# Loading the late slots' rows as runs with SP and turning them on VectorE, instead of gathering them with GpSimd and turning them on TensorE, in a fused attention and mixture-of-experts kernel

## The chip, the cores and the metric

The kernel runs on one core of one Trainium2 chip. The metric is device time in microseconds of one execution. The kernel before took 610.86 us (median of 3 runs, 610.16 to 613.93). The engines are called PE (TensorE matmuls; PEld is its weight load), DVE (VectorE), ACT (ScalarE), POOL (GpSimd) and SP (SyncE, which here only issues DMAs).

## The reference

Linear attention gives 4608 tokens of 512 features. Each token goes to one of 8 experts, the one with the largest cosine similarity, and gets that expert's two-layer network times its gate weight.

```
def _moe_ref(x, expert_emb, tau, w1, w2):
    ...                                   # xn, en: rows over their norms
    logits = xn @ en.T / tau
    expert_idx = np.argmax(logits, axis=1)
    ...                                   # probs: softmax of logits
    gate_w = probs[np.arange(N), expert_idx]
    for e in range(E):
        mask = expert_idx == e
        ...
        h = np.maximum(x[mask] @ w1[e], 0.0)
        out[mask] = gate_w[mask, None] * (h @ w2[e])
```

Here N is 4608, D 512, E 8 and F 1024: W1 of an expert is 512x1024, W2 1024x512, 2 MB each in 4-byte numbers.

## The kernel before, in words

**Two halves.** The first half computes attention and routing for four groups of 1152 tokens. Each token's 512 features, its number and its gate weight (514 words, `DX`) are scattered by POOL into a DRAM table `x_by_e`, in which every expert owns a stretch of `CAP` rows (L689 `scatter`). While that goes on, six early slots of 256 tokens each run through an expert; a list of step names written out by hand (`ORDER`) sets the order there. What the early slots don't take is worked off in late slots of up to 384 tokens (3 tiles of 128), one expert each. With this routing there are ten late slots: seven of 3 tiles and three of fewer, which run the 2-tile code. Their loop is at L1139; all engines run through it in program order, with branches on the slot's count of tokens.

**One late slot `s`**, in the order of the loop:
- `fetch` (L884) of the next slot: `tokens` (L897) has POOL gather the next slot's 384 rows from the table with three indirect DMAs, by a list of places computed ahead; `weights1` (L910) has SP load the next expert's W1 in four column chunks of 512 KB. Each chunk's DMA waits until the chunk before it in that buffer has been split.
- `hidden` (L1156), once as 3-tile and once as 2-tile code, takes four chunks `c` of 256 hidden units: `split2` (W2's chunk into a high and a low part: ACT casts, DVE subtracts), then `ffn1` (L953): 24 matmuls on PE, then the ReLU's high part on ACT (`hh`, L969) and its low part on DVE (`hl`, L971). Every product is done as three matmuls: high by high, high by low, low by high.
- `prepare` (L1166): the next slot's token numbers, SP's loads of the next W2, and `prepx` (L942): 12 PE transposes of 128x128 that turn the gathered rows so that features lie on partitions, then the split of these into `xh` (ACT) and `xl` (DVE). Then `split1` of the next W1: chunks 0 and 1 here, 2 and 3 after the first tile of `ffn2`.
- `ffn2` (L976), per tile: 24 matmuls into one PSUM bank, in the order of the chunks `c`, so that chunk 3's `hh` and `hl` are read by the last six; ACT scales by the gate weight (`ob`, L993) and POOL scatters the rows to the output (L995).

**Around the first late slot**, `last_early` (L1098) does the same by hand for the last early slot: a matmul `spread` broadcasts the places, four DVE instructions (`late_places`, L822) make the list, POOL gathers, PE turns.

Rows of the table behind an expert's last token have never been written; the gather skips them through an index out of range.

Of the kernel before, what the change touches and what calls it, by code (L numbers as in the profile page):

```python
# [9 lines left out]
F32 = mybir.dt.float32  # L10
# [12 lines left out]
E, F = 8, 1024  # L23
# [7 lines left out]

DX = DM + 2
TS = 3
T = TS * P
CAP = N
ROWS = E * CAP
# [24 lines left out]

PAD_LEFT, PAD_RIGHT, PAD_LATE = 88, 184, 176

# [58 lines left out]
lp9.3 lp10.3 lp11.3 x5l0.4 sc2.3 lp12.3 lp13.3 x5l1.4 sc3.3 lp14.3 lp15.3 lp16.3 lp17.3 sc4.3 lp18.3 ob41.4 lp19.3  # L122
lp20.3 lp21.3 lp22.3 sc5.3 lp23.3 lp24.3 lp25.3 lp26.3 sc6.3 lp27.3 lp28.3 lp29.3 lp30.3 lp31.3 sc7.3 lp32.3 lp33.3
sc8.3 od41.4 right.4
# [4 lines left out]
def attention_moe(ctx, tc, q, k, v, emb, tau, w1, w2, out):  # L129
# [44 lines left out]

    x_by_e = dram.tile([ROWS, DX], I32, name="x_by_e")

# [6 lines left out]
    for m, n in ((const, PAD_LEFT), (att["right"], PAD_RIGHT)):  # L183
        POOL.memset(m.tile([P, n], F32, name="pad"), 0.0)
    lower = const.tile([P, P], F32, name="lower")
    half = const.tile([P, GT], F32, name="half")
# [562 lines left out]
    def late_plan():  # L749
# [22 lines left out]
        total = t([1], "total", I32)  # L772
        start_count = t([2, n], "start_count")
        over = const.tile([P, n, TS], U32, name="late_over")
        place = const.tile([P, n, TS], U32, name="late_place")
# [3 lines left out]
        def spread():  # L779

            b["t"] = ps.tile([P, 2, n], F32, tag="t", name="spread")
            PE.matmul(b["t"], ones[:n, :], start_count, start=True, stop=True)
            b["st"], b["ct"] = (b["t"][:, k].unsqueeze(2).broadcast_to([P, n, TS]) for k in range(2))

        plans[-1] = (lambda k, i: par[i : i + 1, k : k + 1], [place, over], total[0:1])
        chain(NG - 1, "lp", [
# [23 lines left out]
            lambda: DVE.tensor_scalar(ft, ft, 0.0, float(P), ALU.max, ALU.mult),  # L810
            lambda: DVE.tensor_scalar(par[:, 0:1], es, float(E - 1), None, ALU.min),
            lambda: DVE.tensor_tensor(ct, ct, ft[:, 1:2], ALU.min),
            lambda: DVE.tensor_tensor(st, st, ft[:, 0:1], ALU.add),
            lambda: DVE.tensor_tensor(ct, ct, ft[:, 0:1], ALU.subtract),
            lambda: DVE.tensor_scalar(bad, es, float(E), float(2 * ROWS), ALU.is_ge, ALU.mult),
            lambda: DVE.scalar_tensor_tensor(ct, bad, -1.0, ct, ALU.mult, ALU.add),
            lambda: DVE.tensor_scalar(par[:, 1:2], ct, 0.0, None, ALU.max),
            lambda: DVE.tensor_scalar(start_count[:, 0], ident[:n, :n], st, None, ALU.mult),
            lambda: DVE.tensor_scalar(start_count[:, 1], ident[:n, :n], ct, None, ALU.mult),
            lambda: DVE.tensor_copy(total, cum[:, E - 1 : E]),  # L820
        ])
        def late_places():  # L822
# [4 lines left out]

        return spread, late_places


    w1f = w1.rearrange("e d f -> (e d) f")
    w2f = w2.rearrange("e f d -> (e f) d")
    raws, w1h, w1l, w2h, w2l, h_t, xs_t, xg_t = [], [], [], [], [], {}, {}, {}
    def h_room(m, name, n):
# [26 lines left out]
    def late_room():  # L861


        close_room("h_early")
        close_room("right")
        m = open_room("late", "right")
        h_room(m, "l", T)
        for i in range(2):
            x_room(m, i, T)
        r2 = [m.tile([P, FC // P, DM], F32, name=f"r2_{c}") for c in range(2)]  # L870
        for i in range(2):
            xg_t[i] = m.tile([P, TS, DX], F32, name=f"xg_{i}")
        raws.append([m.tile([P, NC1, FC], F32, name=f"r1_{c}") for c in range(NF)])
        raws.append(r2 + [m.tile([P, FC // P, DM], F32, name=f"r2_{c}") for c in range(2, NF)])
        DVE.memset(m.tile([P, PAD_LATE], F32, name="pad_late"), 0.0)
        DVE.memset(xg_t[0], 0.0)
# [7 lines left out]
    def fetch(s, plan, i):  # L884
# [3 lines left out]
        ix, xg = ix_t[s % 3][:, :nt], xg_t[set_of(s)]  # L888
        r1, r2 = [[None] * NF, [None] * NF] if s < EARLY else raws

# [6 lines left out]
        def tokens():  # L897
            for j in range(nt):
# [4 lines left out]
                tc.add_to_no_dep_group("gather", ins.ins)  # L903

        def numbers():
# [20 lines left out]
        return ix, xg, r1, r2, (tokens, numbers, weights1, weights2)  # L926

# [14 lines left out]
    def prepx(s, js, got, xs):  # L942

        xg, ts_ = got[1], slice(js[0] * P, (js[-1] + 1) * P)
        xh, xl = (x[:, :, ts_] for x in xs)
        pt = ps.tile([P, NC1, len(js) * P], F32, tag="t" if len(js) == 1 else "x", name=f"pt{s}_{js[0]}")
        for i, j in enumerate(js):
            for c in range(NC1):
                PE.transpose(pt[:, c, i * P : (i + 1) * P], xg[:, j, c * P : (c + 1) * P], ident)  # L949
        yield  # L950
        yield from split(pt, xh, xl)

    def ffn1(s, nt, xs, c):  # L953
# [144 lines left out]
    def last_early():  # L1098

        s, got, gn = EARLY - 1, gots[EARLY - 1], fetch(EARLY, plans[-1], 0)  # L1100
        tokens, numbers, weights1, weights2 = gn[4]
        weights1()
# [10 lines left out]
        go(2, first[0])  # L1113
        spread, places = late_places
        spread()
# [3 lines left out]
        places()  # L1119
        tokens()  # L1120
        go(1, first[0])
        go(2, first[1])
# [7 lines left out]
        for _ in range(3):  # L1130
            go(1, *x)
        DVE.memset(xg_t[1], 0.0)
        go(3, *second)
# [4 lines left out]
    with ExitStack() as ifs:  # L1138
        for s in range(EARLY, SLOTS):  # L1139
# [26 lines left out]
            def prepare(cs, x):  # L1166
                if not last:
                    with late(i + 1):  # L1168
# [44 lines left out]
```

## Time and profile before

| | |
|---|---|
| time, median of 3 runs | 610.86 us |
| time of the profiled execution | 612.98 us |
| its span, first to last instruction | 611.2 us |
| mean granted TensorE clock | 0.963 |
| PE busy | 544.4 us (89%) |
| DVE busy | 330.3 us (54%) |
| ACT busy | 280.2 us (46%) |
| POOL busy | 198.5 us (32%) |
| DMA, mean over the span | 177 GB/s |

How to read the profile: a row of the timeline is start, duration, engine, line, operation, output and input tile, and in brackets how long the engine had been idle before it and what ended that. Matmuls overlap (the next starts before the last has ended), so the pace of PE is read from the starts, not from durations. A row of groups gives count, total busy time, mean duration in nanoseconds, and the idle time before the group. The chain of waits is followed back from the last instruction. Names such as `xg`, `pt`, `w1l`, `ph` are the program's tiles: gathered rows, their transposes in PSUM, W1's low part, `ffn1`'s result in PSUM.

### The profile page before, as it was taken

How to read it: one execution, taken by the hardware profiler on the slowest of the kernel's cores; microseconds unless marked ns; L12 is line 12 of the kernel's file. 1: busy time of each engine (PE TensorE's matmuls, PEld its weight loads, DVE VectorE, ACT ScalarE, POOL GpSimd, SP SyncE). 2: the span in 40 equal slices, each digit the busy share in tenths (PEclk: the TensorE clock that was granted, in tenths of full speed). 3: DMA queues.
4: the chain of work that ended last, by engine and by line, in shares of the span. 5: the costliest groups of instructions: out<-in, count | busy, mean ns of one | idle time of the engine just before them, and what ended most of it. 6: DMA issues, size and time to landing. Idle time of an engine off the chain costs nothing. (4 is left out here: it accounts for less than half of the span.)

```text
span 611.2 us, 13218 instructions
## 1 busy us (share of the span) xinstructions
PE 544.4 (89%) x5170; PEld 489.3 (80%) x5170; DVE 330.3 (54%) x597; ACT 280.2 (46%) x420; POOL 198.5 (32%) x189
## 2 busy tenths in 40 slices
PE   0485627999999999997999999999999999999995
PEld 0364626988888988896998988989898999989894
DVE  5987658783475624763453656624445353624450
ACT  2767536713567414613353646534344352534340
POOL 2645425675514564161403121021130303022111
PEclk9988776999999999998999999999999999999998
DMA  9954875478623422048835576555555535454100
GB/s 321 396 214 157 296 241 174 136 283 247 240 81 115 148 90 103 3 187 310 273 126 178 178 245 196 177 185 189 179 172 159 186 127 176 150 187 159 46 18 31
DMA packets 61043, 108.16 MB, mean 177 GB/s; under 512 B 4350, under 2 KB 29982, under 8 KB 60960
## 3 DMA queue, kind: packets, MB, share of 16 engines
q1 hardware_dynamic: 51600, 78.65, 38.6%
q0 software_dynamic: 9280, 28.40, 12.8%
q8 instruction: 51, 0.84, 0.6%
q14 instruction: 32, 0.26, 0.1%
q10 hardware_dynamic: 80, 0.02, 0.0%
HBM read 89.71 MB, written 19.44 MB: 179 GB/s over the span
## 5 line engine op out<-in xcount | busy, mean ns | idle before, releaser
L995 POOL DMA_INDIRECT out_dram<-ob,ix x38 | 39.2, 1031 | 268.3 <-ACT ob L993 237.8
L964 PE MATMUL ph<-x,w1h 128*128 128x384 f32 (+1 forms) x320 | 102.2, 320 | 2.3 <-ACT ob L993 1.4
L966 PE MATMUL ph<-x,w1l 128*128 128x384 f32 (+1 forms) x320 | 102.1, 319 | 0.0
L965 PE MATMUL ph<-x,w1h 128*128 128x384 f32 (+1 forms) x320 | 102.1, 319 | 0.0
L931 DVE TENSOR_TENSOR w2l<-r,w2h 128x1024 fp32r<-128x1024 f32 x44 | 53.9, 1224 | 72.8 <-ACT w2h L929 72.8
L986 PE MATMUL po<-w2h,h_l 128*128 128x512 f32 x224 | 89.3, 399 | 0.1
L987 PE MATMUL po<-w2l,h_l 128*128 128x512 f32 x224 | 88.1, 393 | 0.0
L988 PE MATMUL po<-w2h,h_l 128*128 128x512 f32 x224 | 88.0, 393 | 0.0
L931 DVE TENSOR_TENSOR w1l<-r,w1h 128x1024 fp32r<-128x1024 f32 x48 | 57.0, 1220 | 39.0 <-ACT w1h L929 39.0
L993 ACT ACTIVATE ob<-po,ix 128x512 f32<-128x512 f32 x38 | 26.1, 687 | 106.9 <-PE po L988 58.0
L971 DVE SCALAR_TENSOR_TENSOR h_l<-ph,h_l 128x768 fp32r<-128x768 f32 (+1 forms) x44 | 37.8, 861 | 63.8 <-ACT h_l L969 63.1
L969 ACT ACTIVATE h_l<-ph 128x768 fp32r<-128x768 f32 (+1 forms) x44 | 32.2, 734 | 86.0 <-issue 62.8
L964 PEld LDWEIGHTS ph<-x,w1h 128*128 128x128 f32 x320 | 60.5, 189 | 3.4 <-ACT ob L993 1.7
L929 ACT CAST w1h<-r 128x1024 fp32r<-128x1024 f32 x48 | 48.4, 1050 | 28.9 <-DMA r<-in_moe_w_dram 28.9
L965 PEld LDWEIGHTS ph<-x,w1h 128*128 128x128 f32 x320 | 60.5, 189 | 0.3
L966 PEld LDWEIGHTS ph<-x,w1l 128*128 128x128 f32 x320 | 60.5, 189 | 0.0
L964 PE MATMUL ph<-x_e,w1h 128*128 128x256 f32 x192 | 55.9, 291 | 0.1
L965 PE MATMUL ph<-x_e,w1h 128*128 128x256 f32 x192 | 54.4, 283 | 0.0
L929 ACT CAST w2h<-r 128x1024 fp32r<-128x1024 f32 x48 | 50.0, 1043 | 9.5 <-PE po L988 4.1
L966 PE MATMUL ph<-x_e,w1l 128*128 128x256 f32 x192 | 54.2, 283 | 0.0
L988 PEld LDWEIGHTS po<-w2h,h_l 128*128 128x128 f32 x224 | 42.6, 190 | 9.2
L986 PEld LDWEIGHTS po<-w2h,h_l 128*128 128x128 f32 x224 | 42.7, 190 | 8.9 <-issue 0.3
(275 smaller groups left out, 1020.0 us busy)
## 6 DMA issues: line engine op xcount, KB each, us to landing
r<-in_moe_w_dram SPq DMA_DIRECT2D x96, 512.0 KB, 4.4
q<-in_q_dram SPq DMA_DIRECT2D x8, 1152.0 KB, 6.2
v<-in_v_dram SPq DMA_DIRECT2D x8, 1152.0 KB, 11.1
k<-in_k_dram SPq DMA_DIRECT2D x7, 1152.0 KB
k<-in_k_dram SPq DMA_DIRECT2D x1, 640.0 KB, 5.4
out_dram<-ob,ix POOLq DMA_INDIRECT x38, 3.2
x_by_e<-x,posu POOLq DMA_INDIRECT x36, 4.7
k<-in_k_dram SPq DMA_DIRECT2D x1, 512.0 KB, 3.9
```

The lines of the kernel that those rows point to most:

```text
L929: ACT.copy(hi, src)
L931: eng.tensor_tensor(lo, src, hi.bitcast(F32), ALU.subtract)
L964: PE.matmul(o, w1h[c][:, d, fs], xh[:, d, :n], start=d == 0, stop=False)
L965: PE.matmul(o, w1h[c][:, d, fs], xl[:, d, :n], start=False, stop=False)
L966: PE.matmul(o, w1l[c][:, d, fs], xh[:, d, :n], start=False, stop=d == NC1 - 1)
L969: ACT.activation(hh[c][:, :, :n], ph[:, :, :n], AF.Relu)
L971: DVE.scalar_tensor_tensor(hl[c][:, :, :n], ph[:, :, :n], 0.0, hh[c][:, :, :n].bitcast(F32), ALU.max, ALU.subtract)
L986: PE.matmul(po, hh[c][:, u, ts_], w2h[c][:, u, :], start=c + u == 0, stop=False)
L987: PE.matmul(po, hh[c][:, u, ts_], w2l[c][:, u, :], start=False, stop=False)
L988: PE.matmul(po, hl[c][:, u, ts_], w2h[c][:, u, :], start=False, stop=c + u == NC2 // 2)
L993: ACT.activation(ob, po, AF.Copy, scale=ix[:, j, 1:2].bitcast(F32))
L995: ins = POOL.indirect_dma_start(out, bass.IndirectOffsetOnAxis(ap=ix[:, j, 0:1], axis=0), ob, None, bounds_check=N - 1, oob_is_err=False,)
```

## The change

The gathers and the PE transposes of all late slots but the first go. In their place:
- `pieces`: SP loads the next slot's rows as they lie, from the first row's place (read into a register), in four DMAs. DMA `c` takes words 128c to 128c+127 of all 384 rows and puts them on partitions 32c to 32c+31, row 32n+r on partition 32c+r, as 12 runs of 512 bytes per partition. A fifth DMA loads the token numbers and gate weights, 8 bytes per row. Then come W1's loads, also in four blocks of 32 partitions with runs of 4 KB (`weights1_parts`), in the order of features that the turned rows have. W1's chunk buffers are now views of one tile, so each of these DMAs waits until all four chunks are split.
- `turnx`: DVE transposes blocks of 32x32, 8 of 12 block columns in chunk 3 of `hidden`, ahead of `ffn1`'s chunk 3, the other 4 in `prepare`; both are then split by ACT and DVE as before, from SBUF instead of PSUM.
- `pad`: since rows behind an expert's end are now read, POOL writes them, two slots ahead, with three indirect DMAs per slot whose other rows are skipped by an index out of range. The table gets 384 more rows per expert and at its end. The list of these places takes four more DVE instructions in the plan, one more small matmul, and four DVE instructions in `last_early` (`behind_places`).

```diff
-CAP = N
+CAP = N + T
...
+        def pad():
+            for j in range(nt):
+                ins = POOL.indirect_dma_start(
+                    x_by_e, bass.IndirectOffsetOnAxis(ap=plan[3][:, i, j : j + 1], axis=0),
+                    early_rows[:, 0].bitcast(I32), None, bounds_check=ROWS + T - 1, oob_is_err=False,
+                )
...
+        def pieces():
+            at = row_at()
+            for c in range(NQ):
+                ins = SP.dma_start(
+                    xq_t[0][c * QB : (c + 1) * QB].bitcast(I32),
+                    at[:, c * P : (c + 1) * P].rearrange("(n r) x -> r n x", r=QB),
+                )
+            ins = SP.dma_start(ix.bitcast(I32), at[:, DM:DX].rearrange("(j p) x -> p j x", p=P))
...
+        def weights1_parts():
+            e = expert()
+            for c in range(NQ):
+                SP.dma_start(
+                    r1_all[c * QB : (c + 1) * QB],
+                    w1f[ds(e * DM, DM), :].rearrange("(q d r) f -> q r d f", q=NQ, d=NC1)[c],
+                )
...
+    def turnx(s, nt, ns, xs):
+        rows = xq_t[0][:, ns.start : ns.stop]
+        ...
+        DVE.transpose(
+            xt.rearrange("p k (n c) -> p n k c", c=QB), rows.rearrange("p n (k r) -> p n k r", r=QB)
+        )
+        yield
+        yield from split(xt, xh, xl)
...
         places()
         tokens()
+        behind_places()
+        fetch(EARLY + 1, plans[-1], 1)[4][4]()
...
-        DVE.memset(xg_t[1], 0.0)
...
-                    gn[4][0]()
-                    gn[4][2]()
+                    gn[4][5]()
+                    gn[4][7]()
+                    if i + 2 < NMAX:
+                        fetch(s + 2, plans[-1], i + 2)[4][4]()
...
                 for c in range(NF):
                     run(split2(c, got))
+                    if c == NF - 1 and not last:
+                        run(turnx(nxt, nt, slice(0, 8), xs_t[set_of(nxt)]))
                     run(ffn1(s, nt, xs, c))
...
-                            gn[4][1]()
                             gn[4][3]()
-                            run(*(prepx(nxt, js, gn, xs_t[set_of(nxt)]) for js in ((0, 1), (2,))))
+                            run(turnx(nxt, TS, slice(8, 12), xs_t[set_of(nxt)]))
                         run(*(split1(c, gn) for c in cs))
+                        if not x:
+                            gn[4][6]()
```

In the last lines `gn[4][0]` is `tokens`, `[1]` `numbers`, `[2]` `weights1`, `[3]` `weights2`, `[4]` `pad`, `[5]` `pieces`, `[6]` `tails` (one DVE instruction that masks the token numbers) and `[7]` `weights1_parts`.

**DVE, at the end of `hidden` and in `prepare` of the first late slot, 2-tile code.** `h_l` with input `ph` is `hl`; `x_37..` is `xl` of the next slot. Before:

```order
L931 TENSOR_TENSOR w2l_718<-r_3_3727,w2h_722 128x1024
L971 SCALAR_TENSOR_TENSOR h_l<-ph_2_3_4190,h_l 128x2x256
L1161 UNCONDITIONAL_BRANCH
L907 TENSOR_TENSOR ix_113<-xg_3721,late_over 128x3
L908 COPY ix_113<-xg_3721 128x3
L931 TENSOR_TENSOR x_3717<-pt_0_4226,x_3717 128x4x256
L931 TENSOR_TENSOR x_3717<-pt_2_4237,x_3717 128x4x128
L931 TENSOR_TENSOR w1l_707<-r_0_3722,w1h_711 128x1024
```

and now:

```order
L991 TENSOR_TENSOR w2l_719<-r_3_3729,w2h_723 128x1024
L1019 STREAM_TRANSPOSE xt_20_4217<-xq 128x8x4x32
L991 TENSOR_TENSOR x_3722<-xt_20_4217,x_3722 128x4x256
L1043 SCALAR_TENSOR_TENSOR h_l<-ph_2_3_4221,h_l 128x2x256
L1238 UNCONDITIONAL_BRANCH
L1019 STREAM_TRANSPOSE xt_38_4255<-xq 128x4x4x32
L991 TENSOR_TENSOR x_3722<-xt_38_4255,x_3722 128x4x128
L991 TENSOR_TENSOR w1l_708<-r_3727,w1h_712 128x1024
```

A transpose and the larger subtraction for `xl` have moved ahead of chunk 3's `hl`; the cast for `xh` has moved ahead of chunk 3's `hh` on ACT in the same way.

**SP, at the top of the same slot.** Before:

```order
L1146 TENSOR_LOAD p_par
L892 TENSOR_LOAD p_par
L915 ISA
L915 DMA r_0_3722<-in_moe_w_dram 128x4x256
L915 ISA
L915 DMA r_1_3723<-in_moe_w_dram 128x4x256
```

and now (the `xq` and `r_3727` rows come four times each):

```order
L1219 TENSOR_LOAD p_par
L925 TENSOR_LOAD p_par
L946 ISA
L946 DMA xq<-x_by_e 32x12x128
...
L951 DMA ix_114<-x_by_e 128x3x2
L911 TENSOR_LOAD p_par
L974 ISA
L974 DMA r_3727<-in_moe_w_dram 32x4x1024
```

Five more DMAs and one more register load stand ahead of W1's four on SP; W2's four follow as before.

**DVE in `last_early`, with the waits that the program sets.** DMASW is a semaphore that a DMA issued by POOL raises. Before:

```order
L825 TENSOR_TENSOR late_place<-number,spread 128x60
L826 TENSOR_TENSOR late_place<-late_place,late_over 128x60 [waits DVE_49]
L971 SCALAR_TENSOR_TENSOR h_l<-ph_2_0_3738,h_l 128x2x256 [waits DMAHW1_49,Activation_49]
L971 SCALAR_TENSOR_TENSOR h_l<-ph_2_1_3765,h_l 128x2x256 [waits Activation_49]
L931 TENSOR_TENSOR w1l_707<-r_0_3722,w1h_711 128x1024 [waits DMAHW6_49,Activation_49]
```

and now:

```order
L834 TENSOR_TENSOR late_place<-late_place,late_over 128x60 [waits DVE_49]
L838 TENSOR_TENSOR xq<-number,spread 128x60 [waits DMASW4_49,DMASW5_49,DMASW3_49,DMASW6_49,DMASW2_49,DMASW7_49,DMASW1_49,DMASW0_49]
L839 TENSOR_SCALAR xq<-xq 128x60 [waits DVE_49]
L840 TENSOR_TENSOR late_behind<-number,spread 128x60
L841 TENSOR_TENSOR late_behind<-late_behind,xq 128x60 [waits DVE_49]
L1043 SCALAR_TENSOR_TENSOR h_l<-ph_2_0_3740,h_l 128x2x256 [waits DMAHW1_49,Activation_49]
```

The first of the four new instructions waits for DMAs that POOL issued, and `hl` of chunks 0 and 1 now stands behind it.

More of the change, by code (lines that the diff above doesn't have):

```diff
@@ L172, in attention_moe @@
         open_room(name, side)
-    x_by_e = dram.tile([ROWS, DX], I32, name="x_by_e")
+    x_by_e = dram.tile([ROWS + T, DX], I32, name="x_by_e")
     ident = const.tile([P, P], F32, name="ident")
@@ L184, in attention_moe @@
         POOL.memset(m.tile([P, n], F32, name="pad"), 0.0)
+    behind = const.tile([P, NSLOT, TS], U32, name="late_behind")
     lower = const.tile([P, P], F32, name="lower")
@@ L779, in spread @@
         def spread():
[L781 to L785, printed above, removed]
+            b["t"] = ps.tile([P, 3, n], F32, tag="t", name="spread")
+            PE.matmul(b["t"][:, :2], ones[:n, :], start_count, start=True, stop=True)
+            PE.matmul(b["t"][:, 2], ones[:n, :], left_n, start=True, stop=True)
+            b["st"], b["ct"], b["left"] = (b["t"][:, k].unsqueeze(2).broadcast_to([P, n, TS]) for k in range(3))
+        plans[-1] = (lambda k, i: par[i : i + 1, k : k + 1], [place, over], total[0:1], behind)
         chain(NG - 1, "lp", [
@@ L819, in late_plan @@
             lambda: DVE.tensor_scalar(start_count[:, 1], ident[:n, :n], ct, None, ALU.mult),
+            lambda: DVE.tensor_scalar(left_n, ident[:n, :n], left, None, ALU.mult),
             lambda: DVE.tensor_copy(total, cum[:, E - 1 : E]),
+            lambda: DVE.tensor_copy(par[:, 2:3], st),
         ])
@@ L826, in late_places, with behind_places @@
             DVE.tensor_tensor(place, place, over, ALU.max)
-        return spread, late_places
+        def behind_places():
+            spare = xq_t[0][:, 0, : n * TS].bitcast(U32).rearrange("p (a b) -> p a b", b=TS)
+            DVE.tensor_tensor(spare, number_n, b["left"], ALU.is_lt)
+            DVE.tensor_scalar(spare, spare, float(OOB), None, ALU.mult)
+            DVE.tensor_tensor(behind, number_n, b["st"], ALU.add)
+            DVE.tensor_tensor(behind, behind, spare, ALU.max)
+        return spread, late_places, behind_places
     w1f = w1.rearrange("e d f -> (e d) f")
     w2f = w2.rearrange("e f d -> (e f) d")
-    raws, w1h, w1l, w2h, w2l, h_t, xs_t, xg_t = [], [], [], [], [], {}, {}, {}
+    raws, w1h, w1l, w2h, w2l, h_t, xs_t, xg_t, xq_t = [], [], [], [], [], {}, {}, {}, []
     def h_room(m, name, n):
@@ L888, in fetch @@
         ix, xg = ix_t[s % 3][:, :nt], xg_t[set_of(s)]
-        r1, r2 = [[None] * NF, [None] * NF] if s < EARLY else raws
+        r1, r2 = [[None] * NF, [None] * NF] if s < EARLY else raws[:2]
+        r1_all = raws[2] if s >= EARLY else None
         def expert():
@@ L903, in tokens, with row_at, tails @@
                 tc.add_to_no_dep_group("gather", ins.ins)
+        def row_at():
+            first = nc.values_load(
+                par(2, i), engines=(mybir.EngineType.SP,), min_val=0, max_val=ROWS,
+                skip_runtime_bounds_check_because="places lie in their expert's rows",
+            )
+            return x_by_e[ds(first, T), :]
+        def pad():
[4 more added lines that the diff above has]
+                )
+                tc.declare_no_dep(ins.ins, group="behind", reason="own rows")
+                tc.declare_no_dep(ins.ins, group="gather", reason="rows behind an expert's last")
+                tc.declare_no_dep(ins.ins, group="pieces", reason="rows behind an expert's last")
+                tc.add_to_no_dep_group("behind", ins.ins)
+        def pieces():
[5 more added lines that the diff above has]
+                )
+                tc.add_to_no_dep_group("pieces", ins.ins)
+            ins = SP.dma_start(ix.bitcast(I32), at[:, DM:DX].rearrange("(j p) x -> p j x", p=P))
+            tc.add_to_no_dep_group("pieces", ins.ins)
+        def tails():
+            DVE.tensor_tensor(ix[:, :, 0], ix[:, :, 0], over[:, i], ALU.max)
         def numbers():
@@ L951, in prepx @@
         yield from split(pt, xh, xl)
+    def turnx(s, nt, ns, xs):
+        rows = xq_t[0][:, ns.start : ns.stop]
+        n = (ns.stop - ns.start) * QB
+        xh, xl = (x[:, :, ns.start * QB : ns.stop * QB] for x in xs)
+        xt = wk.tile([P, NC1, FC], F32, tag="raw", bufs=2, name=f"xt{s}_{nt}{ns.start}")[:, :, :n]
+        DVE.transpose(
+            xt.rearrange("p k (n c) -> p n k c", c=QB), rows.rearrange("p n (k r) -> p n k r", r=QB)
+        )
+        yield
+        yield from split(xt, xh, xl)
     def ffn1(s, nt, xs, c):
@@ L1113, in last_early @@
         go(2, first[0])
-        spread, places = late_places
+        spread, places, behind_places = late_places
         spread()
```

23 lines of the change are left out of this document (15 added, 8 removed).

## The prediction

> **What bounds the kernel now.** I read the busy time by stretches first, one late slot per stretch, then the list of waits of the late part, then the timeline at the seam between `ffn1` and `ffn2`. The stretches (columns: us, then busy time of PE, PEld, DVE, ACT, POOL, then granted clock, DMA share, GB/s) for two 3-tile slots and one 2-tile slot:
>
> ```profile
> 391.70:426.00 34.30, 34.30 (x181) 31.46 (x180) 15.19 (x16) 14.45 (x17) 6.69 (x6) 1.00 0.51 170
> 426.00:460.40 34.40, 34.40 (x183) 31.49 (x181) 15.20 (x16) 14.46 (x17) 6.70 (x6) 1.00 0.51 169
> 366.60:391.70 25.10, 23.75 (x135) 22.42 (x134) 15.21 (x17) 12.87 (x15) 4.05 (x4) 1.00 0.63 207
> ```
>
> PE is busy all of a 3-tile slot at the full clock; VectorE is busy under half of it, ACT as little, DMA half. What PE waited for from 284 us on:
>
> ```profile
> PE pt L949 <- DMA xg<-x_by_e,late_place: 3.7, 3, 2.6
> PE ph L964 <- ACT ob L993: 1.4, 1, 1.4
> PE ph L964 <- ACTq L1179: 1.0, 1, 1.0
> ```
>
> These 6.1 us are the first late slot's gather (3.7) and the ends of two 2-tile slots. Between them PE sets the pace, so an instruction taken off PE shortens the run by its own time, as long as nothing else comes late. The seam in a 3-tile and in a 2-tile slot:
>
> ```profile
> 563.24 0.34 PE L966 MATMUL ph<-x,w1l 128*128 128x384 f32 x1
> 563.41 1.47 PE L949 MATMUL pt<-ident,xg 128*128 128x128 f32 x12
> 564.64 0.48 PE L986 MATMUL po<-w2h,h_l 128*128 128x512 f32 x1
> ...
> 366.64 1.47 PE L949 MATMUL pt<-ident,xg 128*128 128x128 f32 x12
> 367.87 0.48 PE L986 MATMUL po<-w2h,h_l 128*128 128x512 f32 x1
> ```
>
> The 12 transposes push `ffn2` back by 1.23 us from start to start, and its first matmul then takes 0.32 instead of 0.23 to the next. The chain of waits gives the two together as its own piece:
>
> ```profile
> 391.86 1.31 PE pt L949 x12
> 426.19 1.31 PE pt L949 x12
> ```
>
> **What is removed.** Of the ten late slots the first keeps its gather and transposes. Nine sets go (L949 has 120 transposes on `xg`, ten times 12): 9 x 1.31 = **11.8 us**, all on PE. GpSimd loses three gathers per slot and gets three writes of the same kind; it waits most of the time, and the rows it writes are needed a slot later. I cost that at nothing.
>
> **What VectorE and ACT get.** Call T0 the moment at which PE could begin `ffn2`: 563.41 in the 3-tile slot above, 366.64 in the 2-tile slot. The new work stands ahead of chunk 3's `hh` and `hl`, and PE reads that `hl` with the 21st matmul of `ffn2`, 20 x 0.23 = 4.6 us after T0. That pace, and that `ffn2` may start without chunk 3, shows in the last slot, which has no transposes now:
>
> ```profile
> 592.49 0.28 PE L966 MATMUL ph<-x,w1l 128*128 128x256 f32 x1
> 592.85 0.60 ACT L969 ACTIVATE h_l<-ph 128x512 fp32r<-128x512 f32 x1 [1.34 <-issue]
> 592.91 0.47 PE L986 MATMUL po<-w2h,h_l 128*128 128x512 f32 x1
> 593.22 0.40 PE L987 MATMUL po<-w2l,h_l 128*128 128x512 f32 x1
> 593.45 0.40 PE L988 MATMUL po<-w2h,h_l 128*128 128x512 f32 x1
> ```
>
> PE starts at 592.91 while chunk 3's `hh` still runs to 593.45. So the question is when `hl` ends. Today's last instruction ahead of it on VectorE, `w2l` of chunk 3, in the two slots:
>
> ```profile
> 561.28 1.23 DVE L931 TENSOR_TENSOR w2l<-r,w2h 128x1024 fp32r<-128x1024 f32 x1
> 365.57 1.23 DVE L931 TENSOR_TENSOR w2l<-r,w2h 128x1024 fp32r<-128x1024 f32 x1 [0.24 <-ACT w2h L929]
> ```
>
> Behind it come, each waiting for the one before: the transpose of 128x1024 (call it X), ACT's cast to `xh`, VectorE's `xl`, then `hl`. Their prices, by the groups with shapes apart:
>
> ```profile
> L929 ACT CAST w1h<-r 128x1024 fp32r<-128x1024 f32 x48 | 48.4, 1050 | 28.9 <-DMA r<-in_moe_w_dram 28.9
> L931 DVE TENSOR_TENSOR w1l<-r,w1h 128x1024 fp32r<-128x1024 f32 x48 | 57.0, 1220 | 39.0 <-ACT w1h L929 39.0
> L971 DVE SCALAR_TENSOR_TENSOR h_l<-ph,h_l 128x768 fp32r<-128x768 f32 x28 | 26.8, 958 | 53.9 <-ACT h_l L969 53.9
> L971 DVE SCALAR_TENSOR_TENSOR h_l<-ph,h_l 128x512 fp32r<-128x512 f32 x16 | 11.0, 690 | 9.9 <-ACT h_l L969 9.2 <-ACTq L1168 0.7
> ```
>
> 3 tiles: 562.51 + X + 1.05 + 1.22 + 0.96 = 565.74 + X, needed at 563.41 + 4.6 = 568.01: no wait while X is under **2.27 us**. 2 tiles: 366.80 + X + 1.05 + 1.22 + 0.69 = 369.76 + X, needed at 371.24: no wait while X is under **1.48 us**. `hh` ends ahead of `hl` in both.
>
> No row shows a VectorE transpose, so X is bounded by what the trace has on as many numbers per partition: from below a fill of 1542 numbers in 1.34 us, which is 0.9 us for 1024; from above the slowest engine on the same shape, GpSimd's subtraction in 2.48 us:
>
> ```profile
> L876 DVE MEMSET xg<- 128x1542 f32 x1 | 1.3, 1343 | 0.3 <-issue 0.3
> L931 POOL TENSOR_TENSOR w2l<-r,w2h 128x1024 fp32r<-128x1024 f32 x4 | 9.9, 2476 | 3.0 <-ACT w2h L929 2.9
> ```
>
> I take 1.22, VectorE's own subtraction on this shape, since a transpose too reads and writes each number once. Then `hl` is ready 1.05 us early in the seven 3-tile slots and 0.26 us early in the 2-tile ones: PE waits 0. With 2.48 it waits 0.21 us in seven slots and 1.00 in three (the last slot runs the transpose too, on rows nobody uses): 4.5 us in all.
>
> The other four block columns come after `hl`: half of X, 0.6, and half of `xh`, 0.6, so that ACT's casts of W1 start 5.6 us after T0 in a 2-tile slot (3.12 + 1.22 + 1.2). Two casts, one `ob` and two casts are 4 x 1.05 + 0.69 = 4.9, VectorE's last subtraction 1.22 more, and W1's split ends under 12 us after T0, against T0 + 11.07 today (572.12 + 2.36 less 563.41):
>
> ```profile
> 572.12 2.36 DVE L931 TENSOR_TENSOR w1l<-r,w1h 128x1024 fp32r<-128x1024 f32 x2 [2.49 <-ACT w1h L929]
> ...
> L993 ACT ACTIVATE ob<-po,ix 128x512 f32<-128x512 f32 x38 | 26.1, 687 | 106.9 <-PE po L988 58.0 <-issue 43.6 <-PEq L1179 4.8
> ```
>
> PE first wants that last chunk when it has done `ffn2` (48 x 0.23 = 11 us) and three chunks of `ffn1`. Cost 0.
>
> **What SP and the queues get.** Per slot W1 takes 512 runs of 4 KB instead of 2048 of 1 KB, and the rows 1536 of 512 bytes plus 384 of 8, instead of 384 of 2 KB: 2432 runs on both sides, for the same bytes. The rows are asked for when the last transpose has read their buffer, about T0 + 5, and are needed 1 us before the next T0. That is 17 us later when a 2-tile slot is next (its period today is 24.98, by the starts of its transposes and of those before, less 1.31) and 27 when a 3-tile slot is. The longest of W1's chunks took 11.4 us from issue to landing:
>
> ```profile
> 341.66 1.47 PE L949 MATMUL pt<-ident,xg 128*128 128x128 f32 x12
> ...
> DMA to landing us min/median/max: 4.2/4.5/11.4
> ```
>
> W1 itself can start only when all four chunks are split, T0 + 12 at the latest, and ACT first reads it 5.6 us after the next T0: 17 us later if that is of a 2-tile slot, 26 if not. The busiest stretch of loads in the late part, 278 to 300 us, moved
>
> ```profile
> DMA packets 5496, 7.39 MB, mean 336 GB/s; under 512 B 271, under 2 KB 4154, under 8 KB 5495
> ```
>
> so 2.1 MB take 6.2 us. Cover of 10 us; W2's loads queue behind, not ahead. Cost 0. [...]
>
> **The first late slot.** VectorE's new wait there is for the last table scatter, since the buffer used as scratch lay under the scattered rows. POOL's row of that scatter, its next gather, which waits for the same landing, and VectorE and PE around it:
>
> ```profile
> 271.65 0.97 POOL L691 DMA_INDIRECT x_by_e<-x,posu  x1 [0.30 <-issue]
> 276.60 1.05 POOL L899 DMA_INDIRECT xg<-x_by_e,late_place  x1 [2.70 <-issue]
> ...
> 268.35 0.14 DVE L823 TENSOR_TENSOR late_over<-number,spread 128x60 uint32<-128x60 f32 x1
> 268.88 0.22 DVE L826 TENSOR_TENSOR late_place<-late_place,late_over 128x60 uint32<-128x60 uint32 x1
> 269.02 0.68 DVE L971 SCALAR_TENSOR_TENSOR h_l<-ph,h_l 128x512 fp32r<-128x512 f32 x1
> ...
> 276.96 0.39 PE L988 MATMUL po<-w2h,h_l 128*128 128x512 f32 x1
> 284.68 0.63 PE L949 MATMUL pt<-ident,xg 128*128 128x128 f32 x4 [2.56 <-DMA xg<-x_by_e,late_place]
> ```
>
> `hl` of chunk 0, done at 269.7 today, will end near 276.6 + 0.75 (four list instructions take 268.35 to 269.1) + 0.68 = 278.0; PE wants it at 276.96 and waits 1.05 us. Behind that, PE waits 2.56 us for the gather today, whose start does not move, so the new wait eats into the old one. Cost 0; if the gather's wait were gone it would cost 1.05 us. The plan's extra instructions (some 0.6 us) end before 276.6 as well.
>
> One small cost: where the last slot's PE passes a branch with nothing to do in it, `ffn2` starts 0.42 us after the last `ffn1` matmul instead of 0.12. Two more slots get such an empty branch: 0 to 0.6 us, I take 0.3.
>
> **The sum.** On the profiled execution (612.98 us, span 611.2): 612.98 - 11.8 + 0.3 = 601.5. That execution lies 2.1 us above the median of the runs, so **599.4 us** for the median, 1.9% less. A measurement of this kernel can tell about 1%, 6 us, from no change.
>
> **The rivals.**
> 1. *The chain over X is a little too long.* X lies between 1.48 and 3.2 us. For it: the 2-tile slots have only 0.26 us to spare, and a transpose was never seen. Against: all VectorE rows on 1024 numbers stand near 1.2. At 2.48: 599.4 + 4.5 = 603.9.
> 2. *W1 comes late.* It needs more than 17 us from the last split to landing, in the two places where a 2-tile slot is next; nearly three times what today's busiest rate gives. At 20 us each costs 3: 605.
> 3. *Slower: VectorE's transpose becomes the bound.* PE waits 7(X - 2.27) + 3(X - 1.48) us in all, which eats the gain at X = **3.2 us**; above that the change loses. At four times 1.22, 4.88 us, it costs 28.5: 628. For it: `hh`, `hl` and all of `ffn2`'s second part stand behind it in order on two engines. Against: the slowest engine needs 2.48.
> 4. *No change.* The time comes back as other waits of PE, say the rows landing after VectorE wants them in every slot, because of their 1536 short runs; 1.05 us late would go unseen, 1.3 more in nine slots costs 11.7: 611. Against: 17 us of cover.
>
> **Chances and range.** Forecast 0.72 (its own range 597.5 to 601.5), rival 1 0.10, rival 2 0.05, rival 3 0.07, rival 4 0.06. Faster by over 1% (under 604.8) are the forecast, rival 1 and part of rival 2: 0.84; within 1%: 0.09; slower: 0.07. The range runs from 596.5 to 606, which takes in both bounds of X (599.1 and 603.9) and rival 2.
>
> **What would show it.** Right: no L949-like transposes on `xg` past the first late slot; 3-tile periods of 33.0 us instead of 34.34; the STREAM_TRANSPOSE on 8 block columns near 1.2 us; no wait of PE on `hl` at chunk 3; `xq` landed long before VectorE reads it; in the first late slot a PE wait near 1 us at `ffn2`'s third matmul and a shorter one at the gather. Wrong: a transpose above 1.5 us, waits of VectorE on `xq` or of ACT on W1's tile, or periods of 34 us with PE idle in them.

## The result, and the profile after

The changed kernel took 604.5 us (median of 11 runs), the kernel before 612.35 us (median of 11). The medians hold some runs with a lower clock; the ratio without them is 0.984, with a 95% interval of 0.980 to 0.988. So the change saves 1.6% (1.2 to 2.0), where 1.9% was forecast, and 604.5 lies inside the range of 596.5 to 606.

The late part, read first. Busy time by stretches of the changed kernel, two 3-tile slots (columns as before: PE, PEld, DVE, ACT, POOL, granted clock, DMA share, GB/s):

```profile
391.30:424.30 33.00, 33.00 (x169) 30.15 (x168) 17.04 (x18) 14.38 (x17) 6.90 (x6) 1.00 0.68 188
424.30:457.30 33.00, 33.00 (x169) 30.16 (x169) 17.03 (x18) 14.38 (x17) 6.90 (x6) 1.00 0.66 177
```

A 3-tile slot now takes 33.0 us instead of 34.3; PE is still busy all of it. VectorE has 1.8 us more in it, and the DMA engines are busy 0.67 of the time instead of 0.51, though they move nearly the same. At the seam nothing stands between `ffn1` and `ffn2` any more:

```profile
556.23 0.33 PE L1038 MATMUL ph<-x,w1l 128*128 128x384 f32 x1
556.41 0.39 PE L1058 MATMUL po<-w2h,h_l 128*128 128x512 f32 x1
```

VectorE's timeline in the 2-tile slot whose `ffn2` starts at 341.34 (T0), from `w2l` of chunk 3 to `hl`:

```profile
340.29 1.22 DVE L991 TENSOR_TENSOR w2l<-r,w2h 128x1024 fp32r<-128x1024 f32 x1 [0.24 <-ACT w2h L989]
341.43 1.24 DVE L1019 STREAM_TRANSPOSE xt<-xq 128x1024 f32<-128x1024 f32 x1
343.78 1.23 DVE L991 TENSOR_TENSOR x<-xt,x 128x1024 fp32r<-128x1024 f32 x1 [1.12 <-ACT x L989]
344.93 0.68 DVE L1043 SCALAR_TENSOR_TENSOR h_l<-ph,h_l 128x512 fp32r<-128x512 f32 x1
```

The new instruction's group, with shapes apart:

```profile
L1019 DVE STREAM_TRANSPOSE xt<-xq 128x1024 f32<-128x1024 f32 x10 | 12.4, 1238 | 0.0
```

X is 1.24 us, and VectorE never waited for the rows (the 0.0 of idle time ahead of it). `hl` ends at 345.61, the 21st matmul is due at 341.34 + 4.6 = 345.94: 0.33 us early. In a 3-tile slot it is 1.1 us early (394.74 against 395.85). What PE waits for after the first late slot has begun:

```profile
PE ph L1036 <- ACT w1h L989: 1.4, 1, 1.4
PE ph L1036 <- ACTq L1257: 1.1, 1, 1.1
PE ph L1038 <- DVE w1l L991: 0.2, 1, 0.2
```

The two waits at the ends of the 2-tile slots are where they were (1.4 and 1.0 before). But behind the 1.4 the clock fell in this execution. Two matmuls of `ffn1` there in the timeline:

```profile
374.51 0.52 PE L1038 MATMUL ph<-x,w1l 128*128 128x384 f32 x1
374.83 0.52 PE L1036 MATMUL ph<-x,w1h 128*128 128x384 f32 x1
```

And the granted clock (after ACT's and POOL's busy time) by stretches:

```profile
374.00:376.00 2.00, 2.00 (x9) 2.00 (x8) 1.89 (x3) 1.36 (x2) 1.18 (x1) 0.58 0.61 100
376.00:378.00 2.00, 2.00 (x8) 2.00 (x8) 1.61 (x3) 1.05 (x1) 0.00 (x0) 0.57 0.08 22
```

Ten matmuls start 0.32 us apart instead of 0.17: 1.6 us lost. For the whole late part I take the time from the first matmul of the first late slot's `ffn1` to the start of the last matmul, in this and later profiles:

| profile | from, to | late part, us | what fell in it |
|---|---|---|---|
| before | 295.80, 603.69 | 307.89 | |
| before, second | 305.01, 612.88 | 307.87 | |
| change | 296.80, 594.96 | 298.16 | half clock, 1.6 |
| change, second | 299.91, 596.48 | 296.57 | |
| change, third | 298.68, 595.09 | 296.41 | |

Without that accident the late part is **11.4 us** shorter; 11.5 was forecast (11.8 - 0.3).

### The profile page after: what moved, and what is told of

Its sections match the earlier page's. It is cut to its first block, busy times and chain, and to the rows that moved or that the text cites. A ratio compares the mean times of both kernels' runs of the same rounds, so it can differ in the third digit from the quotient of the medians.

```text
span 602.6 us, 13156 instructions
## 1 busy us (share of the span) xinstructions
PE 538.7 (89%) x5064; PEld 483.6 (80%) x5064; DVE 346.4 (57%) x615; ACT 280.9 (47%) x421; POOL 205.0 (34%) x192
## 3 DMA queue, kind: packets, MB, share of 16 engines
q0 software_dynamic: 9520, 24.46, 11.8%
## 5 line engine op out<-in xcount | busy, mean ns | idle before, releaser
L1067 POOL DMA_INDIRECT out_dram<-ob,ix x38 | 42.3, 1113 | 248.6 <-ACT ob L1065 205.7
L1060 PE MATMUL po<-w2h,h_l 128*128 128x512 f32 x224 | 87.3, 390 | 0.0
L1058 PE MATMUL po<-w2h,h_l 128*128 128x512 f32 x224 | 87.3, 390 | 0.0
L1037 PE MATMUL ph<-x_e,w1h 128*128 128x256 f32 x192 | 55.9, 291 | 2.6 <-issue 2.6
L1036 PE MATMUL ph<-x_e,w1h 128*128 128x256 f32 x192 | 57.5, 299 | 0.2 <-ACT et L550 0.2
L1038 PE MATMUL ph<-x_e,w1l 128*128 128x256 f32 x192 | 55.9, 291 | 0.8 <-issue 0.8
```

The source lines that it names most:

```text
L1036: PE.matmul(o, w1h[c][:, d, fs], xh[:, d, :n], start=d == 0, stop=False)
L1037: PE.matmul(o, w1h[c][:, d, fs], xl[:, d, :n], start=False, stop=False)
L1038: PE.matmul(o, w1l[c][:, d, fs], xh[:, d, :n], start=False, stop=d == NC1 - 1)
L1058: PE.matmul(po, hh[c][:, u, ts_], w2h[c][:, u, :], start=c + u == 0, stop=False)
L1060: PE.matmul(po, hl[c][:, u, ts_], w2h[c][:, u, :], start=False, stop=c + u == NC2 // 2)
L1067: ins = POOL.indirect_dma_start(out, bass.IndirectOffsetOnAxis(ap=ix[:, j, 0:1], axis=0), ob, None, bounds_check=N - 1, oob_is_err=False,)
```

## The experiments

**The PE transposes put back.**

```diff
                             gn[4][3]()
+                            for js in ((0, 1), (2,)):
+                                next(prepx(nxt, js, gn, xs_t[set_of(nxt)]))
                             run(turnx(nxt, TS, slice(8, 12), xs_t[set_of(nxt)]))
```

> The changed kernel with the 12 PE transposes put back at their old place in all nine slots (on the first late slot's rows; nobody reads the results). Theory (the change gains PE's own time and nothing else): each set costs 1.31 us again, and the last slot's empty branch on PE returns (0.3 to 0.4 us), so 604.5 + 9 x 1.31 + 0.4 = 616.7, between 0.995 and 1.01 of the time before; 3-tile periods 34.3 us. Rival (the gain came from the gathers that left GpSimd and the DMA queues, or from the first late slot): the time stays under 608, 0.99 or less of before, although PE has its old work.

Measured: 619.57 us, 1.010 (1.005 to 1.014) of before. One of its seams, as it was in the kernel before:

```profile
562.25 0.34 PE L1038 MATMUL ph<-x,w1l 128*128 128x384 f32 x1
562.42 1.47 PE L1009 MATMUL pt<-ident,xg 128*128 128x128 f32 x12
563.65 0.48 PE L1058 MATMUL po<-w2h,h_l 128*128 128x512 f32 x1
```

The late part is 308.36 us, within 0.5 of the kernel before: PE's own time accounts for the gain, and the rival that the gain came from gathers, queues or the first late slot falls. The times as a whole lie 3 to 9 us above before, at the upper end of what was expected; the profiled execution, the fastest of the eight, has the span of before (611.2 us), so no trace shows where the others lost it.

**VectorE's transpose done twice, and four times.**

```diff
-        DVE.transpose(
-            ...
-        )
+        for _ in range(2 if ns.start == 0 else 1):
+            DVE.transpose(
+                ...
+            )
```

> The changed kernel with VectorE's transpose of 8 block columns done twice into the same tile. The trace of the changed kernel shows chunk 3's hl ending 1.11 us ahead of the 21st matmul of ffn2 in a 3-tile slot (394.74 against 395.85) and 0.33 us ahead in a 2-tile slot (345.61 against 345.94). Theory: one more transpose of 1.24 us makes PE wait 0.13 us in seven slots and 0.91 us in three, 3.6 us in all: 608.1. Rival (VectorE has more room than that, because ffn2 doesn't stand on this hl so closely): no PE wait at the 21st matmul, time as the change's, 604.5 within 2 us.

> The same transpose four times, so the chain ahead of hl is 3.72 us longer, near the 4.88 us at which the prediction saw the change lose. Theory: PE waits 2.61 us in seven slots and 3.39 us in three at the 21st matmul, 28.4 us in all, and more if the granted clock falls behind these waits: 633 or more, 1.03 to 1.06 of before; 3-tile periods 35.6 us. Rival (the wait shows only in part because ACT and the splits of W1 catch up elsewhere): under 622.

Twice: 610.37 us, 0.990 (0.986 to 0.993), about 3.4 us over the change. Matmuls 20 and 21 of `ffn2` in a 3-tile slot of it:

```profile
434.51 0.39 PE L1060 MATMUL po<-w2l,h_l 128*128 128x512 f32 x1
434.97 0.50 PE L1061 MATMUL po<-w2h,h_l 128*128 128x512 f32 x1
```

The start comes 0.46 us after the one before instead of 0.23, the next is 0.1 late too, and most 3-tile periods are 33.4 us instead of 33.0; `ffn2` of a 2-tile slot takes 1.2 us more (11.88 against 10.68 in the last slot). I expected 0.13 and 0.91: the place was right, and a wait costs some 0.3 us more than the difference of end and start. The late part is 304.34 us, 7.9 over the change's: 7 x 0.38 and 3 x 1.2, and 1.7 for half clock behind the one-tile slot, as in the first profile of the change.

Four times: 655.36 us, 1.063 (1.054 to 1.072), 48 us over the change, where 28 and "more if the clock falls" were expected. Matmuls 18 to 21 at a 3-tile seam:

```profile
493.32 0.39 PE L1061 MATMUL po<-w2h,h_l 128*128 128x512 f32 x1
495.37 0.50 PE L1059 MATMUL po<-w2h,h_l 128*128 128x512 f32 x1 [1.66 <-ACT h_l L1042]
495.71 0.40 PE L1060 MATMUL po<-w2l,h_l 128*128 128x512 f32 x1
496.79 0.50 PE L1061 MATMUL po<-w2h,h_l 128*128 128x512 f32 x1 [0.68 <-DVE h_l L1044]
```

The stretches behind them:

```profile
497.00:499.00 2.00, 2.00 (x6) 1.56 (x6) 1.06 (x3) 1.62 (x3) 0.00 (x0) 0.59 0.22 37
499.00:501.00 2.00, 2.00 (x7) 1.53 (x6) 2.00 (x2) 2.00 (x3) 0.25 (x1) 0.56 1.08 242
```

The waits are (495.37 - 493.32 - 0.23) + (496.79 - 495.71 - 0.23) = 2.7 us, as expected (2.61). But 0.6 us after them the clock is halved for 3.4 us, which costs about 1.7 more: the period is 37.55 us, 4.5 over the change's. So it goes in six of the seven 3-tile slots, and a wait of 2.7 us costs 4.4 there; in the seventh, whose `ffn2` starts at 415.92, the clock stays at 1.00 behind the same waits, and `ffn2` takes 19.0 us instead of 20.7. The late part is 349.55 us.

**W1's loads over 128 partitions.**

```diff
-                    r1_all[c * QB : (c + 1) * QB],
-                    w1f[ds(e * DM, DM), :].rearrange("(q d r) f -> q r d f", q=NQ, d=NC1)[c],
+                    r1_all[:, c, :],
+                    w1f[ds(e * DM, DM), :].rearrange("(q d r) f -> q r d f", q=NQ, d=NC1)[:, :, c, :],
```

> The changed kernel with W1's four loads cut the other way: each over 128 partitions with one run of 4 KB per partition, instead of 32 partitions with four such runs; same bytes, same run length, same waits. Theory (W1's shape is hidden): the time stays within 2 us of the change's 604.5, 0.98 to 0.99 of before, PE's waits in the 2-tile slots stay. If loads into 32 partitions are slower, the DMA engines' busy share in the late part falls from 0.8 towards the 0.6 of the kernel before at the same GB/s, and the time still stays. Rival (W1 is late in the 2-tile slots because of its shape, which would explain part of the 2 us lost there): the time falls by 1.5 to 3 us and PE's 1.4 us wait for w1h goes.

Neither the theory nor the rival: 663.25 us, 1.080 (1.073 to 1.087). Stretches with W1 alone in flight:

```profile
378.00:379.00 1.00, 1.00 (x11) 1.00 (x10) 0.55 (x1) 0.36 (x1) 1.00 (x1) 1.00 0.26 102
379.00:380.00 1.00, 1.00 (x11) 1.00 (x10) 0.69 (x1) 1.00 (x2) 0.39 (x1) 1.00 0.27 103
```

ACT's first cast of that W1:

```profile
401.96 1.99 ACT L989 CAST w1h<-r 128x1024 fp32r<-128x1024 f32 x2 [15.16 <-DMA r<-in_moe_w_dram]
```

About a quarter of the DMA engines' time is used, and W1, asked for at 372.12, is not there until 401.96. The source's outermost step has four entries, and 4 of the 16 engines would be a share of 0.25; in the change that step has 32 entries, and the share with W1 in flight is 1.02 to 1.06 (rows below). That the four entries confine the load is my reading of these rows; no run varied that step alone. The experiment changed that step without meaning to, and can't answer its own question; but it shows rival 2 of the prediction at work: the late part is 356.86 us, 60 over the change's, and ACT waits for W1 for 59.2 us in it. In the change itself the rate of W1 can be read directly, by stretches (356 to 360 us W1 and little else, 366 to 368 W2 behind it):

```profile
356.00:357.00 1.00, 1.00 (x11) 1.00 (x10) 0.47 (x1) 0.27 (x1) 0.53 (x1) 1.00 1.02 201
358.00:360.00 2.00, 1.90 (x16) 1.70 (x15) 1.28 (x2) 0.30 (x2) 1.70 (x2) 1.00 1.06 219
366.00:368.00 2.00, 2.00 (x11) 1.64 (x10) 0.89 (x2) 1.19 (x2) 0.00 (x0) 1.00 1.04 375
```

And W1 alone in the kernel before, in two slots:

```profile
378.00:379.00 1.00, 1.00 (x7) 1.00 (x7) 0.77 (x1) 0.20 (x1) 0.00 (x0) 1.00 1.02 352
398.00:400.00 2.00, 2.00 (x10) 1.66 (x9) 0.00 (x0) 1.27 (x2) 0.31 (x1) 1.00 0.94 287
```

By these rows (GB/s over DMA share), fully busy DMA engines move about 200 GB/s into 32 partitions, and 305 to 360 into 128. W1, asked for from 352.72 on, is in at 365.2, where its last transfer of 4 KB ends in the trace; ACT reads it at 370.9, so 5.7 us of cover are left. The rows of the load over 128 partitions, whose runs are of 4 KB too, bear on the run length: 102 GB/s at a share of 0.26 are 390 per full share, so the runs are not what is slow, though only about a quarter of the engines' time was used there.

**W1's loads in 16 DMAs, the four blocks in turn.**

```diff
-            for c in range(NQ):
-                SP.dma_start(
-                    ...
+            for d in range(NC1):
+                for c in range(NQ):
+                    SP.dma_start(
+                        r1_all[c * QB : (c + 1) * QB, d],
+                        w1f[ds(e * DM, DM), :].rearrange("(q d r) f -> q r d f", q=NQ, d=NC1)[c, :, d],
+                    )
```

> The changed kernel with W1's load cut into 16 DMAs, each one run of 4 KB on 32 partitions, taking the four blocks of partitions in turn instead of one block after the other. In the changed kernel W1 alone moves 193 to 234 GB/s with the DMA engines fully busy (355 to 366 us), W2 behind it 375 to 385. Theory (a block of 32 neighbouring partitions takes only about 0.6 of the rate, and W1 is hidden all the same): with the blocks in turn W1 moves at over 300 GB/s or SP's 16 issues of 0.45 us (7 us) become its limit, 290 GB/s; the late part stays 296.5 us when no accident of the clock falls in it, and the time is the change's within 1%. Rival (the runs of 4 KB themselves are slow): W1 stays at 220 GB/s and below. Second rival (full DMA engines hold up program code and so cost time in every execution): the median falls by 3 us or more.

Measured: 607.01 us, 0.978 (0.970 to 0.987); late part 296.44 us, as the change's. W1 in flight:

```profile
361.00:363.00 2.00, 2.00 (x20) 2.00 (x18) 1.39 (x2) 1.27 (x2) 1.50 (x2) 1.00 1.01 258
365.00:367.00 2.00, 2.00 (x17) 1.82 (x16) 1.13 (x2) 2.00 (x4) 0.00 (x0) 1.00 0.83 236
```

SP's 16 issues take 10 us (first to last) and set the pace, so it is no faster as a whole; per full share it moves 255 to 285 GB/s in these stretches and 220 to 300 in the next slot, instead of about 200. That speaks for the 32 neighbouring partitions as the limit, and not for the runs of 4 KB, without being a clean measurement. The second rival isn't borne out: the late part is the same, and the ratio can't be told from the change's. Whether W1 comes in four blocks one after the other or in turns costs the run nothing.

**The turn one chunk earlier; PE kept busy at the seam.** The first two of three experiments on the waits at the ends of the 2-tile slots. The edits:

```diff
                 for c in range(NF):
+                    if c == NF - 2 and not last:
+                        turns = [turnx(nxt, nt, ns, xs_t[set_of(nxt)]) for ns in (slice(0, 8), slice(8, 12))]
+                        ...
                     run(split2(c, got))
-                    if c == NF - 1 and not last:
-                        run(turnx(nxt, nt, slice(0, 8), xs_t[set_of(nxt)]))
```

```diff
-                with tc.If(cnt > j * P):
+                with tc.If(cnt > j * P) as more:
                     run(ffn2(s, j, got))
+                if j == 1:
+                    with more.Else():
+                        keep_on(100 + i, 13)
```

> The changed kernel with VectorE's transposes of all 12 block columns and their split moved one chunk earlier, ahead of chunk 2's split of W2, so that nothing of it lies between hl of chunk 3 and W1's split. Theory (what the change lost in the slot of one tile is the wait for W1's split, 1.42 and 0.17 us, and the half clock behind it, 1.6): W1's split starts about 2 us earlier after ffn2's start, the wait shrinks below 0.5 us, the clock stays at 1.00 there, and the late part is 3 us shorter: 601.5, about 0.976 of before. In the 2-tile slots hl of chunk 3 ends within 0.2 us of the 21st matmul. Rival (the clock falls there for another reason, or the rows or W1 land too late for the earlier use): the late part stays within 1 us of the change's 298.2 us, or grows with waits on xq or W1's tile.

> The changed kernel with 13 PE matmuls of 128x128 (1.3 us, results unused) where a slot has one tile only, in the time in which PE waits for W1's split. Nothing is faster by itself. Theory (the half clock follows PE's idle time): the clock stays near 1.00 behind them and the slot after is 1.6 us shorter, the wait for w1h nearly gone from PE's list; late part 296.5 us. Rival (the clock falls for another reason, or the wait itself is the cost): late part 298 us or more.

Beside them the change itself ran again: 600.41 us, 0.987 (0.978 to 0.996).

> The changed kernel itself once more, beside the variants on one chip. Theory (the gain is PE's 9 x 1.31 us less the half clock behind one wait): 0.98 to 0.988 of before, 3-tile periods 33.0 us, and in the slot of one tile again a PE wait of 1.4 us for w1h followed by some 3.4 us at a granted clock near 0.57. Rival (that clock dip was an accident of one execution): the wait returns without the dip, and the time from the first late slot's ffn1 to the last matmul is 296.5 us instead of 298.2.

Its wait of 1.4 us is there again and no clock dip behind it (late part 296.57 us), and in the third profile the same: the rival holds, the dip comes in some executions and not in others. PE kept busy (605.39 us, 0.995, 0.991 to 1.000) therefore tells little: the clock stayed at 1.00 behind the added matmuls, but it did so without them too, and the 13 ran as 26 rows in 3.06 us, where a wait of 1.4 was to be filled. Its late part is 302.19 us: the time from that slot's last `ffn2` matmul to the next `ffn1` grew from 1.81 to 4.13 us, and PE stopped for 2.4 us in the `ffn1` of the slot before, with half clock behind it:

```profile
336.67 0.39 PE L1038 MATMUL ph<-x,w1l 128*128 128x256 f32 x1 [2.26 <-issue]
```

The early turn took 605.41 us, 0.993 (0.987 to 0.999): no gain. Its late part is 301.44 us, 5 more than the change's, and the long stop below, with half clock behind it, is more than all of that: that slot's `ffn1` takes 17.02 us, against 11.7 to 11.8 in the change. PE's waits in its late part:

```profile
PE ph L1037 <- issue: 3.8, 1, 3.8
PE ph L1036 <- ACT ob L1065: 1.5, 1, 1.5
PE ph L1036 <- ACTq L1259: 1.1, 1, 1.1
```

The stretches in which the long one falls:

```profile
356.00:358.00 2.00, 0.19 (x2) 0.00 (x0) 0.80 (x1) 0.00 (x0) 1.36 (x1) 1.00 1.03 201
358.00:360.00 2.00, 0.00 (x0) 0.00 (x1) 0.00 (x0) 0.00 (x0) 0.00 (x0) 1.00 1.02 266
```

W1's split is done at 372.1 there, 3 us before PE starts `ffn1` at 375.06, and the wait is still 1.5 us: W1's split was not its cause, my theory of it falls. From 356 to 358 VectorE and GpSimd end what they have, from 358 to 360 nothing runs on any engine, and the DMA engines are full all the time. What lands in that time on the queues that the profile calls `instruction`, which I take to bring program code (packets, MB, share):

```profile
q8 instruction: 1, 0.02, 4.3%
q14 instruction: 1, 0.01, 1.9%
```

PE stops 5.1 us into that slot's `ffn1`, behind its 43rd matmul, and at the same matmul in the nested variant below (3.7 us) and in the kernel with four transposes (3.5 us). In the change it stumbles there by 0.2 to 0.4 us (358.63 to 359.00 instead of 0.12 apart); in the kernel before not at all. The first row is one packet of 0.02 MB; in the trace of the change every packet of that queue has 16 KB (50, 0.82 MB). I call one a block of code.

The stops end alike in the traces: PE starts again 1.4 to 1.5 us after such a block's transfer has ended (358.53, PE at 360.00), and so it does in the nested variant (361.87, 363.33), with four transposes (376.66, 378.09), behind the stop with PE kept busy (335.28, 336.67) and behind the stumble in the change (357.62, 359.00). What the runs add is when the block comes: SP asked for W1 2.4 us ahead of this `ffn1` (348.36 against 350.80), and the block's transfer began 6 us into it; in the change 0.8 us ahead (352.72 against 353.52), and the block came 3 us in (356.25). With four transposes and in the nested variant it was 3.2 and 2.7 us, and both blocks came 6 us in. I take it that the block queues behind W1 in the DMA engines, and that the early turn, by letting SP ask sooner, made PE wait for it. That is an estimate from these times, and no run tried it by itself; the stop with PE kept busy doesn't fit it, since W1 was asked for 5.7 us ahead of that `ffn1` (324.69 against 330.42), as in the change, where nothing stopped there.

**The third tile's branch inside the second's**, on the kernel with the early turn.

```diff
-            for j in range(1, TS):
-                with tc.If(cnt > j * P):
-                    run(ffn2(s, j, got))
+            with tc.If(cnt > P):
+                run(ffn2(s, 1, got))
+                with tc.If(cnt > 2 * P):
+                    run(ffn2(s, 2, got))
```

> The kernel with VectorE's turn one chunk earlier, and the branch for a slot's third tile moved inside that for its second, so that a slot of one tile passes one branch that is not taken instead of two. There the earlier turn left a PE wait of 1.50 us although W1's split was long done. Theory (that wait is the passing of branches not taken, 1.1 us after one as in the slot of two tiles and some 0.4 for each more): the wait at the end of the slot of one tile falls from 1.5 to about 1.1 us, that of the slot of two tiles stays 1.1. Rival (PE waits there for ACT's scaling of the tile, ob): it stays 1.4 to 1.5.

Measured: 605.64 us, 0.991 (0.986 to 0.996); late part 301.21 us, with the stop above in it. PE's waits:

```profile
PE ph L1037 <- issue: 3.7, 1, 3.7
PE ph L1036 <- ACTq L1260: 1.4, 1, 1.4
PE ph L1036 <- ACT ob L1065: 1.1, 1, 1.1
```

The wait of the one-tile slot fell from 1.5 to 1.1, the theory's number, though the profile still puts it down to `ob`. That of the two-tile slot, forecast to stay, rose from 1.1 to 1.4; it now leaves two nested branches, which would explain it. In these two runs the waits follow the branches, one branch 1.1 us and a second 0.3 to 0.4 more; ACT's `ob` has ended 0.3 to 0.7 us before PE starts (377.67 against 377.99, and 374.35 against 375.06 with the early turn alone).

**A second profile of the kernel before, a third of the change.**

> A second profile of the kernel before. Theory (stops of PE without a wait that the program sets come from the DMA engines being full while program code is fetched, and before they are full less): no such stop after 284 us, late part (first late ffn1 to the last matmul) 307.9 us within 0.5. Rival (they are accidents that hit either kernel): a stop of 2 to 4 us with half clock behind it in the late part of this one too.

> A third profile of the changed kernel, beside the second of the kernel before. Without an accident the late part is 296.6 us, as in the second; a clock dip behind the wait in the slot of one tile adds 1.6, a stop for program code with its half clock 4 to 6. Theory: the waits of 1.1 and 1.4 us at the ends of the two slots with fewer tiles are there again, as they are in the kernel before.

Before: 622.23 us, no stop in the late part (307.87 us), but stops of PE ahead of it, in the last early slot's `ffn1`, with half clock behind them:

```profile
281.51 0.28 PE L965 MATMUL ph<-x_e,w1h 128*128 128x256 f32 x1 [0.87 <-issue]
283.64 0.37 PE L966 MATMUL ph<-x_e,w1l 128*128 128x256 f32 x1 [1.13 <-issue]
285.76 0.37 PE L966 MATMUL ph<-x_e,w1l 128*128 128x256 f32 x1 [1.04 <-issue]
```

The first profile of the change has such stops at 272 to 276 us, its second has none. They hit either kernel. From that `ffn1` to the first late slot's it takes 31.3 and 30.6 us before, 31.0, 30.0 and 30.9 with the change: where the stops come, the gather's wait is gone, and the other way round. What starts them isn't settled. They are not stops behind a block of code as above, as the expectation had it: in this profile no such block is transferred between 266 and 288 us. The third profile of the change: 604.57 us, late part 296.41 us, both waits there.

## Why the prediction was right, point by point

- **The bound, and the 11.8 us.** PE set the pace of the late slots, and an instruction taken off it shortened the run by its own time: the 3-tile periods fell by 1.31 to 1.33 us, and putting the transposes back brought 308.36 us.
- **X.** Taken as 1.22, bounded by 0.9 and 2.48; it is 1.24. `hl` was forecast 1.05 and 0.26 us early, and is 1.1 and 0.33. One transpose more makes PE wait, so the limits were real. Rivals 1, 3 and 4 didn't come (VectorE's idle time ahead of its transposes is 0.0); with four transposes rival 3 did, at more than its price: the prediction summed only waits, and the half clock behind a wait of 2.7 us adds 1.7.
- **The empty branch, +0.3.** Wrong in sign. With no work for PE in it, PE has no branch there at all. Before, the last slot's `ffn2` started 0.42 us after `ffn1`'s last matmul; now every one starts 0.12 to 0.18 after, and with the transposes put back the last slot has 0.43 again. It saved 0.4.
- **The 2-tile slots.** Not foreseen: the two in the middle and the 3-tile slot behind them gave back 0.77 us of their 3.9 (slot by slot from the third profile, 1.21, 1.08 and 0.87 instead of 1.31). The branch wait is 0.1 longer, PE stumbles 0.2 at the matmul of the long stop, and `ffn1` behind the one-tile slot starts 0.44 slower (375.86 to 376.37 for one matmul in the second profile), for `w1l`. 11.8 - 0.77 + 0.4 is the measured 11.4. That it lies so near the forecast 11.5 is luck: the 0.77 that nobody foresaw and the 0.7 by which the branch term was off cancel.
- **The transfers.** Cost 0 was right, the reason half right. 6.2 us for W1 and 10 us of cover were taken from the rate into 128 partitions. Measured are 12.5 us and 5.7. The change loads W1 into 32 partitions at a time, and with W1 alone that ran at about 200 GB/s with the DMA engines full, 0.6 of the 336 GB/s that the 6.2 us were taken from.
- **The first late slot.** The net was right, nothing; the PE wait of 1.05 us at `ffn2`'s third matmul didn't show. In the second profile `hl` of chunk 0 ends at 282.5 and that matmul is due at 282.6, because the last scatter landed 4.0 us after its start and not the 4.95 that the gather's row suggested. The gather's wait shrank from 2.56 to 1.82 us.
- **The size.** 1.9% was forecast, 1.6% measured, inside the interval. The late part delivered the forecast. Of what lies between, 1.6 us are half clock in the profiled execution of the change. The rest isn't found: the first late `ffn1` starts at 295.8 and 305.0 us in the profiles before and at 296.8, 299.9 and 298.7 with the change, which is no difference clear of its spread. But with PE's transposes put back the time came out 1.0% above before, though the late part was longer by 0.5 us only; so the changed kernel may lose some us elsewhere, in executions that no profile caught.

## What to carry to other kernels

Where one engine is busy all of a stage at its full clock, price a change there by that engine's own time and check each other engine only against the moment at which the busy one reads its result: a slack of 0.3 us, read from the starts of the matmuls, held. Look at the stretch with the least slack and at the fullest queue before moving work earlier: what is done sooner also starts its transfers sooner. Here SP asked for W1 1.6 us sooner, and PE stopped for 3.8 us in the next `ffn1`; that a block of code queued behind W1 is my estimate for it. A PE wait can cost more than itself, by half clock behind it: a wait of 2.7 us cost 4.4 in six slots of seven, and one of 1.4 us cost 1.6 more in one profile of the change out of three.

## What the runs showed of the hardware

- VectorE's transpose in blocks of 32x32 on 4-byte numbers takes 1.24 us for 128x1024 and 0.70 for 128x512 in the change (means of 10 and 9), as much as its subtraction on these shapes (1.23 and 0.69).
- W1's loads into 32 neighbouring partitions moved about 200 GB/s per full share of the DMA engines (201 at 1.02, 219 at 1.06), loads into 128 partitions 305 to 360 (287 at 0.94, 352 at 1.02, 375 at 1.04). The load whose source's outermost step has four entries moved 102 to 103 GB/s at a share of 0.26 to 0.27.
- PE stopped for 3.5 to 3.8 us at one matmul in three variants, while next to nothing ran elsewhere, and started again 1.4 to 1.5 us after the transfer of a 16 KB packet on a queue called `instruction` had ended; with W1 asked for 1.6 to 2.4 us later it cost 0.2 to 0.4 us at the same place, and in the kernel before nothing. That the packet was late because of W1's loads is argued, not shown.
- PE waits of 1.4 to 1.6 us at one seam were followed by half clock in the first profile of the change and with the transpose done twice, and not in the change's next two profiles nor with W1 in 16 DMAs. The dip at this seam lasts 3.4 us (374.31 to 377.73 in the trace of the change), and every stretch of half clock in the traces of before and of the change, but for the last in each, lasts 3.41 us or a multiple of it. What decides whether one follows the wait isn't shown.
